# One addition of every output pair moved from VectorE to an accumulating DMA, the seven products of a pair reordered, and two weight loads moved ahead of the parameters

## The chip, the cores and the metric

The kernel runs on one core of a Trainium2 chip. The metric is the device time of one execution in microseconds (us). The kernel before takes 205.03 us, the median of three runs (203.96 to 205.6).

In profile lines PE is TensorE, PEld its weight loads, DVE is VectorE, ACT is ScalarE, POOL is GpSimd and SP is SyncE. A "q" behind the name (POOLq, SPq) is that engine's sequencer, which issues DMAs. L690 is line 690 of that kernel's own text, so the same statement can have different numbers in two kernels.

## The reference

Input x is 2048 tokens of 512 channels. Everything runs on its layer norm:

```python
xn  = layernorm(x)
u   = xn @ B_bar.T                     # complex, 512 states
h_t = Lam_bar * h_(t-1) + u_t          # scan over the 2048 tokens
y   = 2 * real(h @ C.T) + xn * Dskip
g   = silu(xn @ w1) * (xn @ w3)        # 1792 wide
out = x + y + g @ w2
```

The kernel works in four blocks of 512 tokens. A block has 14 tiles of gates (w1 and w3, called `glu`), 4 complex tiles of scan input (`bu`), and two output pairs. A pair is 256 tokens by 512 columns of the output. Gates and scan states are the contraction of one matrix product: 22 slices of 128.

## The kernel before

A pair is multiplied by a Strassen-like scheme: the left operand is cut into A11, A12, A21, A22 (128 tokens by 11 slices of 128, so 128x1408 each), and seven products of 11 matmuls of 256 columns replace eight. The price is four sums of left operands, each 128x1408, on VectorE:

```python
def row_sums(n, b, p):                       # cut
    return [(0.9, ... tensor_tensor(out=out, in0=x, in1=z, op=op), ("sums", n))
            for out, x, z, op in ((s1, a21, a22, ALU.add),        # S1 = A21 + A22
                                  (a21, a11, a21, ALU.subtract),  # S3 = A11 - A21
                                  (s2, s1, a11, ALU.subtract))]   # S2 = S1 - A11
```

The products, in program order (cut):

```python
def y_fast(n, then=()):
    mms(g, v["a11"], weight(0, D1), True)                 # 1  A11
    copy(f, g)
    bg.fill()
    mms(t, v["s1"], tsum[0], False, cols)                 # 2  S1, into PSUM tile t
    copy(q[1][:, cols], t)                                #    ScalarE takes it out
    bg.first(list(then))                                  #    the next pair's sums go to the front
    mms(f, v["a12"], weight(1, D1), False)                # 3  A12
    nc.vector.tensor_tensor(out=v["s4"], in0=v["a12"], in1=v["s2"], op=ALU.subtract)
    mms(g, v["s2"], tsum[1], False)                       # 4  S2
    mms(z, v["a22"], tsum[3], True)                       # 5  A22
    mms(t, v["s4"], weight(1, D2), False, cols)           # 6  S4, into tile t again
    product7()                                            # 7  S3
```

Between the products `bg.fill()` emits waiting VectorE tasks (sums, scans, scan products) as far as a simple count of TensorE's and VectorE's time allows. An argument of `bg.fill` holds VectorE's tasks back. `steps()` emits the next piece of a ScalarE list.

Near the first two pairs, the third block is made ready:

```python
def ln_scalar_engine(...):                     # layer norm of block 2 on ScalarE
    ...                                        # squares on ScalarE, then on GpSimd:
    gp.tensor_scalar(out=ss, ...)              #   L278
    gp.tensor_tensor(out=rstd, ..., op=ALU.pow)#   L279
    gp.tensor_tensor(out=nb, ...)              #   L280
  def norm(cl):
    nc.scalar.activation(out=xn_blk[b][:, cl, :], ...)    # L285, waits for L280
    ln_transpose(b, cl)                        # a DMA: xnT <- xn, four per block

def pre_c():                                   # scan input of the second block
    gp.dma_start(out=st["g"], in_=st["p"], accum_op=ALU.add)     # u <- p, 512 KB
```

And the head, in which the parameters of the scan are loaded ahead of the weights of the third and fourth gate tiles:

```python
load_w(0, 2 * P)
for i, src in enumerate((A_log_dt, A_Lambda_re, A_Lambda_im)):
    nc.sync.dma_start(out=par_rows[i * NPT:(i + 1) * NPT, :], in_=...)
load_w(2 * P, 4 * P)
```

## Time and profile before

| stretch of TensorE's program | us | length |
|---|---|---|
| head, to the first matmul of 512 columns | 0 to 13.47 | 13.47 |
| gates and scan inputs of blocks 1 and 2 | 13.47 to 70.45 | 56.98 |
| output pairs 0 and 1 ("the stretch" below) | 70.45 to 87.27 | 16.82 |
| gates of the third block to the last matmul | 87.27 to 200.08 | 112.81 |

The page of the kernel before, cut to its busy line, two of the slice rows (each digit is the busy tenths of 1/40 of the span; PEclk is the clock that TensorE was granted) and the two large DMA queues:

```profile
PE 198.3 (98%) x1317; PEld 122.8 (60%) x1317; DVE 172.7 (85%) x242; ACT 125.4 (62%) x251; POOL 39.0 (19%) x65
...
PEclk9999999999999999999999999999999999999999
DMA  6899999992573042926796004466330780101011
...
q1 hardware_dynamic: 25512, 13.21, 27.9%
q0 software_dynamic: 2592, 9.44, 24.9%
```

TensorE is busy for 198.3 of 203.1 us at full clock, VectorE for 85%. The view by windows, one row for each stretch of the table above (busy us of each engine, instructions in brackets; then granted clock, DMA share and GB/s):

```profile
13.47:70.45 56.98, 56.98 (x268) 25.83 (x265) 53.53 (x74) 52.13 (x101) 16.69 (x20) 1.00 0.75 164
70.45:87.27 16.82, 16.82 (x156) 15.06 (x155) 16.10 (x24) 13.30 (x34) 4.34 (x7) 1.00 0.57 110
87.27:200.08 112.81, 112.81 (x774) 73.64 (x771) 93.64 (x123) 51.63 (x96) 11.67 (x14) 1.00 0.38 76
```

In all three rows PE's busy time equals the length: there is nothing but matmuls. The waits of PE, longest first, of that profile (us in total, times, longest):

```profile
PE bu_ps L557 <- DMA w_sb<-in_B_w_dram: 1.0, 1, 1.0
PE bu_ps L193 <- PEq L883: 0.8, 1, 0.8
```

The only wait with a cause in the kernel's order is 1.0 us for weights in the head. Last, the timeline of GpSimd and then of ScalarE around the first pair (start, us, engine, line, operation, tiles; in brackets how long the engine had idled and for what):

```profile
72.55 0.89 POOL L468 DMA_DIRECT2D u<-p  x1 [3.21 <-DVE u L461]
74.73 0.80 POOL L278 TENSOR_SCALAR acc<-acc 128x4 f32<-128x4 f32 x1 [1.29 <-ACT xn L275]
75.61 1.05 POOL L279 TENSOR_TENSOR rstd_all<-acc,mhalf 128x4 f32<-128x4 f32 x1
76.74 0.25 POOL L280 TENSOR_TENSOR acc<-acc,rstd_all 128x4 f32<-128x4 f32 x1
80.42 0.93 POOL L468 DMA_DIRECT2D u<-p  x1 [3.43 <-DVE u L461]
```

```profile
73.56 0.36 ACT L744 ACTIVATE x_blk<-bu_ps 128x256 f32<-128x256 f32 x1
...
77.03 2.93 ACT L285 ACTIVATE xn<-x_blk,acc,rstd_all 128x512 bf16<-128x512 bf16 x4 [2.12 <-POOL acc L280]
```

GpSimd's chain L278, L279, L280 ends at 76.99, and the four layer norms of L285 start at once.

### The profile page before, as it was taken

What the parts mean: (1) busy time and instruction counts of PE and PEld (TensorE: products, weight loads), DVE (VectorE), ACT (ScalarE), POOL (GpSimd) and SP (SyncE); (2) the same over time, 40 slices, a digit from 0 to 9 for tenths busy, and PEclk for the clock granted to TensorE, in tenths of its full rate; (3) what the DMA queues carried; (4) which work ended last, traced back from release to release, by engine and by line L of the source; (5) the groups of instructions that cost most, each with busy time, mean ns of one, the idle gap of its engine ahead of it and who ended that gap; (6) DMA issues with size and microseconds to landing.
All of it is one profiled execution on the core that took longest, in us unless ns stands there. A gap on an engine that the chain in (4) does not pass through costs nothing.

```text
span 203.1 us, 3444 instructions
## 1 busy us (share of the span) xinstructions
PE 198.3 (98%) x1317; PEld 122.8 (60%) x1317; DVE 172.7 (85%) x242; ACT 125.4 (62%) x251; POOL 39.0 (19%) x65
## 2 busy tenths in 40 slices
PE   8899999999999999999999999999999999999994
PEld 2784444444444488854444445888444458888993
DVE  3779699999999999989949999999999935584832
ACT  4699897699999977959766676110566662101010
POOL 3250269700310143021111010310101110000000
PEclk9999999999999999999999999999999999999999
DMA  6899999992573042926796004466330780101011
GB/s 173 248 247 191 312 203 106 350 281 42 101 146 66 0 90 57 183 86 118 68 194 131 13 13 94 91 143 132 90 65 0 149 162 2 52 3 52 29 40 39
DMA packets 28696, 23.16 MB, mean 114 GB/s; under 512 B 16008, under 2 KB 26376, under 8 KB 28680
## 3 DMA queue, kind: packets, MB, share of 16 engines
q1 hardware_dynamic: 25512, 13.21, 27.9%
q0 software_dynamic: 2592, 9.44, 24.9%
q10 hardware_dynamic: 576, 0.30, 0.5%
q8 instruction: 10, 0.16, 0.3%
q14 instruction: 6, 0.05, 0.1%
HBM read 7.74 MB, written 2.10 MB: 48 GB/s over the span
## 4 chain that ended last, share of the span: by engine, by line
PE 93%; DMA 3%; SPq 2%; DVE 1%; issue 0%
PE gu_ps L525 45%; PE gu_ps L724 16%; PE y_ps L724 9%; PE bu_ps L724 7%; PE bu_ps L435 7%; PE y_ps L435 7%; DMA w_sb<-in_B_w_dram 3%; PE gu_ps L557 1%; PE bu_ps L557 1%; DVE xn L735 1%; SPq L166 0%; SPq L151 0%; SPq L161 0%; SPq L152 0%; DVE x_blk L735 0%
## 5 line engine op out<-in xcount | busy, mean ns | idle before, releaser
L525 PE MATMUL gu_ps<-xnT,w_sb 128*128 128x512 bf16 x424 | 92.5, 379 | 0.0
L525 PEld LDWEIGHTS <-w_sb 128*128 128x128 bf16 x424 | 41.4, 98 | 49.4
L724 PEld LDWEIGHTS <-act 128*128 128x128 f16 x451 | 43.2, 98 | 5.5
L534 ACT ACTIVATE g<-gu_ps 128x512 bf16<-128x512 f32 x55 | 33.1, 602 | 14.6 <-PE gu_ps L525 14.4
L535 ACT ACTIVATE u<-gu_ps 128x512 bf16<-128x512 f32 x55 | 33.2, 603 | 9.8 <-PE gu_ps L525 9.5
L543 DVE TENSOR_TENSOR act<-g,u 128x1024 f16<-128x1024 bf16 x28 | 19.0, 677 | 4.4 <-ACT u L535 4.4
L435 PEld LDWEIGHTS <-bt 128*128 128x128 bf16 x128 | 12.5, 98 | 15.1
L478 DVE TENSOR_TENSOR_SCAN u<-rho,act,u 128x512 bf16<-128x512 f32 x16 | 19.6, 1266 | 0.0
L492 POOL DMA_DIRECT2D act<-p x8 | 7.2, 900 | 45.8 <-DVE act L488 31.8
L435 PE MATMUL bu_ps<-xnT,bt 128*128 128x512 bf16 x64 | 15.1, 379 | 0.0
L435 PE MATMUL y_ps<-xnT,bt 128*128 128x512 bf16 x64 | 15.1, 379 | 0.0
L457 DVE TENSOR_TENSOR p<-u,tabe 128x2048 bf16<-128x2048 bf16 x8 | 9.8, 1219 | 2.6 <-DMA act<-p 2.5
L724 PE MATMUL y_ps<-tw,act 128*128 128x256 f16 x88 | 10.9, 272 | 0.0
L437 ACT ACTIVATE u<-y_ps 128x512 bf16<-128x512 f32 x16 | 9.5, 595 | 2.3 <-PE y_ps L435 2.1
L724 PE MATMUL gu_ps<-w_sb,act 128*128 128x256 bf16 (+1 forms) x84 | 10.8, 268 | 0.0
L724 PE MATMUL gu_ps<-tw,act 128*128 128x256 f16 x88 | 10.7, 273 | 0.0
L437 ACT ACTIVATE u<-bu_ps 128x512 bf16<-128x512 f32 x16 | 9.5, 595 | 2.0 <-PE bu_ps L435 1.9
L468 POOL DMA_DIRECT2D u<-p x6 | 5.3, 878 | 26.8 <-ACT u L535 7.9
L744 ACT ACTIVATE bu_ps<-y_ps 128x256 f32<-128x256 f32 x4 | 1.5, 369 | 13.7 <-PE y_ps L724 13.7
L461 DVE TENSOR_TENSOR u<-u,tabe 128x2048 bf16<-128x2048 bf16 x8 | 9.8, 1220 | 0.2
L478 DVE TENSOR_TENSOR_SCAN u<-rho,ends,u 128x512 bf16<-128x512 f32 x8 | 9.9, 1268 | 0.0
L484 DVE TENSOR_TENSOR p<-u,tabe 128x2048 f16<-128x2048 bf16 x8 | 9.8, 1221 | 0.1
(143 smaller groups left out, 275.1 us busy)
## 6 DMA issues: line engine op xcount, KB each, us to landing
act<-p POOLq DMA_DIRECT2D x8, 512.0 KB, 4.7
u<-p POOLq DMA_DIRECT2D x6, 512.0 KB, 4.7
xn<-x_blk POOLq DMA_DIRECT2D x4, 512.0 KB, 5.6
out_dram<-xn SPq DMA_DIRECT2D x15, 128.0 KB, 1.7
w_sb<-in_B_w_dram SPq DMA_DIRECT2D x1, 1792.0 KB
x_blk<-in_A_x_dram SPq DMA_DIRECT2D x3, 512.0 KB, 9.0
w_sb<-in_B_w_dram SPq DMA_DIRECT2D x2, 768.0 KB, 7.1
w_sb<-in_B_w_dram SPq DMA_DIRECT2D x4, 256.0 KB, 3.7
```

The lines of the kernel that those rows point to most:

```text
L435: nc.tensor.matmul(out=ps, lhsT=bt[:, ri, dt, pt * P:(pt + 1) * P], rhs=xnT_blk[b][:, dt, :], start=(dt == 0), stop=(dt == NDT - 1))
L437: nc.scalar.activation(out=u[:, j, ri, :], in_=ps, func=ACT.Copy)
L457: nc.vector.tensor_tensor(out=st["p"][:, :, ::-1, :], in0=st["g"], in1=tabe[:, psl, 2:0:-1, :], op=ALU.mult)
L461: nc.vector.tensor_tensor(out=st["g"], in0=st["g"], in1=tabe[:, psl, 0:1, :].to_broadcast(FULL), op=ALU.mult)
L478: nc.vector.tensor_tensor_scan(out=v, data0=rho[:, pt:pt + 1].to_broadcast([P, TBLK]), data1=v, initial=init, op0=ALU.mult, op1=ALU.add)
L484: nc.vector.tensor_tensor(out=st["p16"][:, :, ::-1, :], in0=st["g"], in1=tabe[:, psl, 1:3, :], op=ALU.mult)
L492: gp.dma_start(out=act_state(b, hf), in_=st["p16"], accum_op=ALU.add)
L525: nc.tensor.matmul(out=ps[:, tsl], lhsT=w[:, dt, f * P:(f + 1) * P], rhs=xnT[:, dt, tsl], start=(dt == 0), stop=(dt == NDT - 1))
L534: nc.scalar.activation(out=g16[:, f % 2, :], in_=g_ps, func=ACT.Silu)
L535: nc.scalar.activation(out=u16[:, f % 2, :], in_=u_ps, func=ACT.Copy)
L543: nc.vector.tensor_tensor(out=act(b)[:, k0:k1 + 1:k1 - k0, :], in0=g16, in1=u16, op=ALU.mult)
L724: nc.tensor.matmul(out=out, lhsT=left[:, k, :], rhs=right[k][:, cols], start=(start and k == 0), stop=(k == NK - 1), skip_group_check=True)
```

## The change

The intent is to take one of the sums from VectorE: S1 = A21 + A22 is made in place of A21 by an accumulating DMA. S3 then needs a place of its own, S2 = A22 - S3, and the product of S1 moves to the fifth place so that its DMA has time. The second part moves two weight loads ahead of the parameters, and TensorE's work on those weights ahead of the parameters' transpose. With them comes a hold-back: over the last three gate tiles of the second, third and fourth block VectorE's waiting tasks are put off. Cut to its core:

```diff
@@ head
     load_w(0, 2 * P)
+    load_w(2 * P, 4 * P)
     for i, src in enumerate((A_log_dt, A_Lambda_re, A_Lambda_im)):
         nc.sync.dma_start(out=par_rows[...], ...)
-    load_w(2 * P, 4 * P)
@@ first block: quarters of the first gate tiles
             quarter(0, (0, 1), 2)
+            quarter(1, (0, 1)); ln_first_transpose(2); quarter(0, (2,)); quarter(1, (2,))
             pps = params_transpose() ... table_angles(1)
-            quarter(1, (0, 1)); ln_first_transpose(2); quarter(0, (2,)) ... quarter(1, (2,))
@@ gates: the hold-back
-            bg.fill()
+            bg.fill(-0.7 if b > 0 and f >= NFT - 3 else None)
@@ row_sums
-    S1, S3, S2 on VectorE
+        return [(0.9, subtract(s3, a11, a21), ("sums", n)),
+                (0.0, lambda: gp.dma_start(out=a21, in_=a22, accum_op=ALU.add), ("sums", n)),
+                (0.9, subtract(s2, a22, s3), ("sums", n))]
@@ y_fast: order of the products
-    A11, S1, A12, S2, A22, S4, S3   (last pair: S3 before S4)
+    A11, A22, A12, S2, S1, S3, S4
@@ before the first pair
+    bg.flush(("ends", 0))
```

## The prediction

> **What bounds the kernel now.** TensorE. The page gives PE 198.3 of 203.1 us at a granted clock of 1.00, and the chain of waits is one unbroken run of matmuls from 9.89 to 198.87 us: 112 matmuls of 512 columns in 24.17 us (216 ns each), 11 of 256 columns in 1.20 us (109 ns). By windows, PE is busy in all of 9.85 to 198.9 us. VectorE is 85% busy but PE never waits for it there. Two places are not matmul: the head, where PE waits 1.0 us (8.88 to 9.89 us) for the third gate tile's w3 weights, and the tail after 198.87 us.
>
> **What the change does.** PE has the same 2636 instructions, so the matmul floor stays. VectorE loses one 128x1408 operation of 0.88 us for each of 8 output pairs, 7 us in all; eight accumulating DMAs of 352 KB from GpSimd replace them, about 4 us each, an estimate from the existing 512 KB ones (4.7 us to landing). The Trainium skill ("DMA: Bandwidth & Descriptors", SWDGE vs HWDGE vs iDMA) says that accumulation is possible only from GpSimd; this trace agrees, all 9.44 MB of it is in the software queue q0. S1's product moves from second to fifth place of seven, 4.8 us into a pair, so the DMA has 6 us or more of slack. VectorE's 7 us are off the critical path: worth nothing.
>
> **Head.** Three small issues (about 1.1 us) leave the SyncE queue ahead of the two weight loads, so the w3 load should land near 8.7 us in place of 9.85 and the 1.0 us wait should shrink to 0 to 0.3 us. But the parameters are now transposed after quarter (1,2), and kr, rho and the 1.28 us table load hang on them: par, dtv, kr, rho, table, first Silu. I put that Silu at 12.1 us (12.56 before), so the first 512-column matmul, which needs its buffer, starts at about 12.9 against 13.47 us. Gain 0.5 us.
>
> **Where it can be given back.** (1) Pair 0: the copy of S1's product now has one product's time before S4 reuses that PSUM, and stands on ACT behind a normalisation that waits for POOL (77.0 us): 0 to 0.4 us. (2) The start of the third block's gates (87.3 us): its last transposes of xn land at about 86.7 us, delayed by an accumulating DMA that fills the 16 DMA engines from 82 to 85 us (DMA share 0.97 to 1.04). The change puts both of that block's accumulations later and two stores ahead of the fourth transpose: 0 to 1 us of wait.
>
> Sum: -0.5, +0.2, +0.3, and 1 and 2 may stay zero: about -0.4 us.
>
> **Prediction: 204.5 us, 8 in 10 between 203.4 and 205.9. Faster by over 2%: 0.01; within 2%: 0.965; slower by over 2%: 0.025.**
>
> **What would show it.** Right: PE's wait for w_sb in the head gone or under 0.3 us, first 512-column matmul at 12.7 to 13.2 us; DVE busy about 166 us; PE busy unchanged within 1 us; no PE wait for the S1 DMA. Wrong: waits of PE for ACT near 77 us, or for xnT near 87 us, over 0.5 us each; a wait of PE for par_rows near 9.4 us.
>
> **What would make it wrong.** Parameters landing after 10 us behind the weights in the same rings; the S1 DMA queueing behind other accumulations by over 6 us; VectorE running late in a pair, since S3's product now waits for an addition with one product's time.

## The result, and the profile after

The changed kernel takes 209.94 us (median of six runs, 209.45 to 211.63) beside 204.5 us (203.85 to 205.6, six runs) of the kernel before. The ratio is 1.0282, 95% interval 1.0226 to 1.0338: slower. Here and below a ratio is the mean time of one kernel's fast runs over that of the other's fast runs of the same rounds, so it is not quite the ratio of the quoted medians. Executions over 1.5% slower than the fastest of the same kernel are left out of the means.

The page after, the same lines as before:

```profile
PE 200.8 (97%) x1317; PEld 124.0 (60%) x1317; DVE 166.6 (80%) x234; ACT 124.8 (60%) x251; POOL 56.3 (27%) x73
...
PEclk9999999999999995799999999999999999999999
DMA  5999995991789068950639784299970087982911
...
q0 software_dynamic: 13984, 12.32, 43.0%
```

VectorE lost 6.1 us of work as intended, the software queue q0 (GpSimd's DMAs) rose from 24.9% to 43.0%, and the clock row, all nines before, has a 5 and a 7 between 78 and 88 us. The three stretches by windows:

```profile
12.43:69.41 56.98, 56.98 (x265) 25.82 (x264) 54.32 (x77) 51.69 (x101) 20.85 (x28) 1.00 0.84 171
69.41:92.25 22.84, 19.87 (x156) 16.58 (x155) 14.41 (x24) 13.30 (x34) 7.59 (x9) 0.85 0.77 98
92.25:205.06 112.81, 112.81 (x774) 73.68 (x771) 91.00 (x118) 51.68 (x96) 23.85 (x20) 1.00 0.63 95
```

The first and the third row are the same to 0.01 us. The stretch of the first two pairs grew from 16.82 to 22.84 us. PE's busy time in it, 19.87 in place of 16.82, says that 3.05 us of that are slower matmuls, and 22.84 - 19.87 = 2.97 us are idle. The head gave 13.47 - 12.43 = 1.04 us in this pair of profiles, so the sum is 6.02 - 1.04 = 4.98 us, against 208.0 - 203.1 = 4.9 us of the spans. The largest wait of PE:

```profile
PE bu_ps L730 <- ACT x_blk L750: 3.0, 1, 3.0
```

Timelines of GpSimd and ScalarE at that place:

```profile
73.03 1.95 POOL L690 DMA_DIRECT2D act<-act  x1 [4.76 <-DVE tw L687]
75.06 1.26 POOL L278 TENSOR_SCALAR acc<-acc 128x4 f32<-128x4 f32 x1
76.40 1.90 POOL L279 TENSOR_TENSOR rstd_all<-acc,mhalf 128x4 f32<-128x4 f32 x1
78.38 0.20 POOL L280 TENSOR_TENSOR acc<-acc,rstd_all 128x4 f32<-128x4 f32 x1
78.60 0.95 POOL L468 DMA_DIRECT2D u<-p  x1
```

```profile
78.61 0.81 ACT L285 ACTIVATE xn<-x_blk,acc,rstd_all 128x512 bf16<-128x512 bf16 x1 [5.02 <-POOL acc L280]
79.33 0.36 ACT L750 ACTIVATE x_blk<-bu_ps 128x256 f32<-128x256 f32 x1
```

The DMA of S1 of the second pair (L690) takes GpSimd 1.95 us to issue, where the u<-p of the kernel before took 0.89. Behind it stands the chain of the layer norm, which ends at 78.58 in place of 76.99. The issue is only a part of that: ScalarE's squares were done at 73.32, so the chain started 1.7 us late behind the issue, and its three steps then took 3.52 us from start to end in place of 2.26. Steps of the same length follow the issue in e3, e4 and e15; why they are longer was not tested. ScalarE waits for the chain with L285, and the copy of S1's product (L750) stands behind that in ScalarE's program. TensorE needs the copied PSUM tile for S4. Then the clock, in windows of 2 us (the DMA share counts the whole time of each packet where it starts, so that a short window can show more than 1):

```profile
77.00:79.00 2.00, 0.00 (x0) 0.00 (x0) 0.73 (x2) 0.39 (x1) 1.90 (x3) 0.97 1.42 106
79.00:81.00 2.00, 1.26 (x7) 0.89 (x7) 0.75 (x2) 2.00 (x4) 0.55 (x1) 0.50 0.59 103
81.00:83.00 2.00, 2.00 (x11) 1.45 (x10) 0.71 (x2) 0.81 (x2) 0.00 (x0) 0.50 0.97 166
83.00:85.00 2.00, 2.00 (x11) 1.42 (x10) 0.84 (x1) 0.37 (x2) 0.86 (x1) 0.50 2.00 70
85.00:87.00 2.00, 2.00 (x17) 1.65 (x15) 0.00 (x0) 2.00 (x8) 0.00 (x0) 0.82 0.93 188
```

TensorE is granted half its clock (0.50) from 78.88 to 85.71 us by the trace's clock records (the expectation of e4 below says 85.3): it is "busy" in these rows and does half the work. The clock fell during the wait, 2.1 us after the last matmul had ended at 76.77, and TensorE resumed at 79.74.

A second delay is hidden in this trace. The four transposes of the third block's xn landed 2.8, 2.4, 5.2 and 4.4 us after their issue before, and take 7.0, 5.5, 6.2 and 3.8 us now; the last lands at 91.4 us in place of 86.7 (the landings that `prof` does not list are read from the semaphore updates in the traces). The gates that need them start at 92.25, so nobody waits. But had the pairs kept their 16.82 us, the gates would have been due at 69.41 + 16.82 = 86.23 us and would have waited up to 5 us, an estimate that leaves the landings where they are.

### The profile page after: what moved, and what is told of

It reads as the page before. It is cut to its first block, busy times and chain, and to the rows that moved or that the text cites. A ratio compares the mean times of both kernels' runs of the same rounds, so it can differ in the third digit from the quotient of the medians.

```text
span 208.0 us, 3442 instructions
## 1 busy us (share of the span) xinstructions
PE 200.8 (97%) x1317; PEld 124.0 (60%) x1317; DVE 166.6 (80%) x234; ACT 124.8 (60%) x251; POOL 56.3 (27%) x73
## 2 busy tenths in 40 slices
DMA packets 40088, 26.04 MB, mean 125 GB/s; under 512 B 27400, under 2 KB 37768, under 8 KB 40072
## 4 chain that ended last, share of the span: by engine, by line
PE 62%; DVE 14%; POOL 9%; issue 8%; DMA 4%; ACT 0%; POOLq 0%
PE gu_ps L525 23%; PE gu_ps L730 16%; PE y_ps L730 7%; PE bu_ps L730 7%; PE bu_ps L435 3%; PE y_ps L435 3%; DMA xn<-x_blk 3%; DVE act L543 2%; DVE stats L214 2%; DVE tw L663 1%; DVE tw L371 1%; DMA x_blk<-in_A_x_dram 1%; DVE ct L397 1%; PE gu_ps L557 1%; POOL act L690 1%
## 5 line engine op out<-in xcount | busy, mean ns | idle before, releaser
L730 PEld LDWEIGHTS <-act 128*128 128x128 f16 x462 | 45.0, 101 | 10.0 <-issue 3.1
L690 POOL DMA_DIRECT2D act<-act x8 | 15.8, 1975 | 23.9 <-DVE tw L687 13.8
L730 PE MATMUL bu_ps<-w_sb,act 128*128 128x256 bf16 (+3 forms) x98 | 13.0, 275 | 3.0 <-ACT x_blk L750 3.0
L730 PE MATMUL gu_ps<-w_sb,act 128*128 128x256 bf16 (+3 forms) x112 | 14.9, 275 | 0.0
L770 DVE TENSOR_TENSOR act<-act,tw 128x1408 f16<-128x1408 f16 x4 | 3.6, 892 | 10.0 <-PE gu_ps L730 8.4
```

The source lines that it names most:

```text
L690: (0.0, lambda: gp.dma_start(out=a21, in_=a22, accum_op=ALU.add), ("sums", n)),
L730: nc.tensor.matmul(out=out, lhsT=left[:, k, :], rhs=right[k][:, cols], start=(start and k == 0), stop=(k == NK - 1), skip_group_check=True)
```

## The experiments

All 18 kernels gave correct results. "Stretch" is from the first product of pair 0 to the first gates of the third block, "rest" from there to the end of the last matmul; both are from one profile. The time is the median of all runs (four each, six for e17, and six of before and of after); the ratio takes the fast ones alone (three each for e5 and e9). All profiled runs were fast, but for e5, whose profiled run is 2% above its fastest and counts as slow: its two lengths and its waits are of that run.

| run | what it is | us | ratio to before (95%) | stretch | rest |
|---|---|---|---|---|---|
| before | | 204.5 | 1 | 16.82 | 112.81 |
| after | the whole change | 209.94 | 1.028 (1.023 to 1.034) | 22.84 | 112.81 |
| e1 | before + head | 205.2 | 1.004 (1.000 to 1.008) | 18.08 | 112.82 |
| e2 | after, S1 of pair 1 issued late | 213.3 | 1.042 (1.034 to 1.049) | 25.18 | 114.45 |
| e3 | after, norms behind the copy | 210.8 | 1.030 (1.025 to 1.035) | 22.31 | 114.51 |
| e4 | after + 28 useless matmuls | 209.14 | 1.023 (1.019 to 1.026) | 21.21 | 112.82 |
| e5 | after, S1 of pair 1 on VectorE | 208.99 | 1.018 (1.011 to 1.025) | 21.27 | 114.51 |
| e6 | after, every S1 on VectorE | 212.06 | 1.037 (1.033 to 1.040) | 22.57 | 114.51 |
| e7 | e5 + GpSimd held 6.9 us | 212.82 | 1.040 (1.038 to 1.043) | 24.91 | 112.82 |
| e8 | e6 with the old head | 208.73 | 1.020 (1.015 to 1.026) | 20.19 | 114.41 |
| e9 | after without hold-back | 209.78 | 1.026 (1.021 to 1.030) | 21.51 | 112.83 |
| e10 | before + hold-back | 205.68 | 1.004 (1.001 to 1.008) | 17.32 | 112.82 |
| e11 | e8 without hold-back | 206.64 | 1.010 (1.009 to 1.012) | 17.76 | 113.93 |
| e12 | before, parameters from GpSimd | 205.14 | 1.003 (1.002 to 1.005) | 16.81 | 112.82 |
| e13 | last six pairs changed, rest before | 204.26 | 1.001 (0.998 to 1.004) | 16.81 | 112.81 |
| e14 | e13 + new head | 205.43 | 1.006 (1.003 to 1.009) | 17.96 | 112.83 |
| e15 | first two pairs changed, rest before | 209.39 | 1.025 (1.021 to 1.029) | 21.78 | 112.82 |
| e16 | e13, VectorE held 6 copies in the head | 205.35 | 1.006 (1.003 to 1.008) | 16.98 | 112.83 |
| e17 | e13 + e12 | 205.04 | 1.004 (1.002 to 1.006) | 16.82 | 112.81 |
| e18 | e13, VectorE held 8 copies | 206.4 | 1.008 (1.006 to 1.011) | 18.16 | 112.82 |

The theory at the outset: GpSimd's long issue delays the layer norm, which delays the copy, which stops TensorE, and the half clock doubles the loss. The rivals: the reordering alone, the head, or the DMA traffic does it.

### e1: the head alone

The edit to the kernel before is the first two hunks of the diff above.

> The kernel before with only the head of the change (weight loads ahead of the parameters, quarters reordered). All theories: the head's share of the change is a gain, since in the trace of the changed kernel the first 512-column matmul starts at 12.43 us against 13.47 us. Expected 1.0 us faster than before: about 203.5 us where before has 204.5, no PE wait for w_sb over 0.3 us, nothing else moved.

205.2 us, ratio 1.004. The wait for w_sb fell to 0.3 us, but new waits came later: 0.7 us for VectorE's S4 subtraction (L766), which starts at 75.7, and 0.2 us for xnT at 87.6. So the head alone is far from the 5 us, and its own gain is gone. e14, e16 and e18 come back to this.

### e2: the DMA of S1 issued behind the layer norm's chain

```diff
+        if late:                 # in y_fast, after the product of A22
+            late()
-    y_fast(0, row_sums(1, *pairs[1]))
+    second = row_sums(1, *pairs[1])
+    y_fast(0, (second[0], second[2]), second[1][1])
```

> The changed kernel with one instruction moved: the accumulating DMA for the second pair's S1 is issued behind the three small POOL operations of the normalisation, not ahead of them. Theory A (POOL's queue: 1.95 us of issuing ahead of the normalisation, the copy of S1's product waits on ACT behind that normalisation, PE waits 3 us and its clock halves for 6 us): PE's wait near 77 us falls from 2.97 us to under 0.3 us, the granted clock stays 1.0, about 203.5 to 204.5 us. Rival B (the accumulating DMAs cost by their traffic and descriptor writing wherever they are issued): stays within 1 us of 209.9 us. Rival C (the new order of products as such): stays at 209.9 us.

213.3 us, the slowest of all. The wait for the copy shrank from 3.0 to 0.8 us, as the theory has it, but TensorE now waits 2.9 us for the S1 DMA itself and 2.5 us for xnT, with half clock after both. The issue can't be moved a few microseconds back without meeting its own deadline.

### e3: the norms behind the copy in ScalarE's program

```diff
-    ln_scalar_engine(2, ..., sins, (0, 1, 4))
+    ln_scalar_engine(2, ..., sins, (0, 1, 5))
```

> The changed kernel with the four normalisations one step later in ACT's program, so that the copy of S1's product stands ahead of them; POOL's order is as in the change. Theory A: PE's wait near 77 us gone although POOL's chain still ends near 78.4 us; but the normalised rows of the third block come as late as in the change while PE arrives 5 us earlier, so PE may wait up to 1.5 us for xnT near 86 us: 203.5 to 205.5 us. Rival B: POOL and the DMA engines as busy as before, so 208 us or more. Rival C: 209.9 us.

210.8 us, not better. PE's waits in this run:

```profile
PE gu_ps L525 <- DMA xnT<-xn: 2.8, 1, 2.8
PE gu_ps L730 <- ACT gu_ps L750: 1.7, 1, 1.7
...
PE y_ps L730 <- DVE x_blk L741: 0.5, 1, 0.5
```

The 3.0 us wait behind the norm is gone; 2.8 us for xnT, 1.7 us for the next copy and 0.5 us for an addition on VectorE stand in its place. The copy's place was a limit, but not the only one.

### e4: TensorE kept at work during the wait

```diff
         for t, cols in halves:
+            # n == 0 only, ahead of the S4 product
+            for _ in range(28):
+                nc.tensor.matmul(out=f, lhsT=ones[:, 0:P], rhs=ones[:, 0:DH], start=True, stop=True)
```

> The changed kernel with 28 useless matmuls of 256 columns (3.05 us at full clock) on PE just ahead of S4's product of the first pair, where PE idles 2.97 us. If the half clock from 79 to 85.3 us comes from that idle time, the clock stays at 1.0 and the half-speed loss of about 3.1 us goes: about 206.8 us. If the clock drops for a reason that has nothing to do with the idle time, 209.9 us. The result stays correct: the matmuls write a PSUM tile that is read no more.

The clock stays at 1.0, yet only about 0.8 us of the 3 us come back: 209.14 us. Two rows of the windows of 2 us:

```profile
80.00:82.00 2.00, 2.00 (x20) 1.67 (x18) 0.78 (x3) 2.00 (x5) 0.39 (x1) 1.00 0.65 119
82.00:84.00 2.00, 2.00 (x21) 1.80 (x19) 1.54 (x2) 1.46 (x4) 0.16 (x1) 1.00 0.98 171
```

In this profile the stretch is 1.6 us shorter than in the change: the useless matmuls fill 3.3 us, and the xnT wait, hidden before, shows with 1.0 us from 90.4. The head of this profile is 0.7 us longer, of the size of its scatter. The half clock is shown as a consequence of the idle time, and the second limit stands close behind it.

### e5, e6, e8: S1 back on VectorE

```diff
-   (0.0, lambda: gp.dma_start(out=a21, in_=a22, accum_op=ALU.add), ("sums", n)),
+   (0.0, lambda: nc.vector.tensor_tensor(out=a21, in0=a21, in1=a22, op=ALU.add), ("sums", n)),
    # e5: for n == 1 only; e6: for all pairs; e8: for all pairs, with the old head
```

> The changed kernel with the S1 of the second pair alone added on VectorE in place; the seven other S1 stay accumulating DMAs. Revised theory: that one DMA does the harm, by holding POOL's queue for 1.95 us ahead of the normalisation and by filling the DMA engines ahead of the two scan accumulations and the transposes of xn. Then PE's wait near 77 us is under 0.5 us, xnT is there near 88 us, clock 1.0, 204 to 206 us. Rival (the harm is spread over all eight DMAs, or lies in the new order): 208 us or more.

> The changed kernel with all eight S1 added on VectorE in place, order of products and head as in the change. If the other seven DMAs are harmless, this equals the run with the second pair alone within 0.5 us, 204 to 206 us. If they cost too, it is over 1 us faster than that run. If VectorE's 0.88 us per pair matters in the new order, it is slower.

> The new order of products alone: all S1 on VectorE, head of the kernel before. If the order as such is harmless it is within 0.7 us of before (204.5 us); if it costs, over 206 us.

e5 has no long issue on GpSimd in the stretch: the wait for the copy is gone, but xnT is waited for 3.6 us. e6 has no S1 DMA at all and is slower than the change itself, 212.06 us, with waits of 4.0 us for xnT and 1.5 us for an addition on VectorE. e8, without the new head, takes 208.73 us:

```profile
PE gu_ps L525 <- DMA xnT<-xn: 2.2, 1, 2.2
PE bu_ps L730 <- ACT x_blk L750: 0.8, 1, 0.8
```

So the DMA isn't the one cause. The order of the products with the hold-back is enough for a loss of 2%, and even with GpSimd's chain on time (ended at 77.08) the copy behind the norm costs 0.8 us. Why the new head makes e6 3 us slower than e8 was followed up only for the head by itself (below).

### e7: GpSimd held without a DMA

```diff
+   hold = [(0.0, lambda: [gp.tensor_copy(out=junk, in_=s3[:, k, :]) for k in range(9)], ...)]  # n == 1
-   return [(0.9, subtract(s3, a11, a21), ("sums", n)),
+   return [(0.9, subtract(s3, a11, a21), ("sums", n)), *hold,      # and S1 of pair 1 on VectorE
```

> As the run with the second pair's S1 on VectorE, with nine small POOL copies [...]where that DMA's issue stood: POOL is held as by the DMA, without its traffic. If POOL's queue is what counts, PE waits near 77 us for 2 to 3 us again, the clock falls, 208 to 210 us. If the traffic in the DMA engines counts, no such wait, 204 to 206 us.

```profile
73.12 6.90 POOL L690 COPY junk<-tw 128x128 f16<-128x128 f16 x9 [4.53 <-DVE tw L688]
...
81.51 0.20 POOL L280 TENSOR_TENSOR acc<-acc,rstd_all 128x4 f32<-128x4 f32 x1
```

```profile
PE bu_ps L733 <- ACT x_blk L753: 5.0, 1, 5.0
```

The copies were meant to hold GpSimd as long as the DMA's issue. They hold it for 6.9 us, far longer than that issue, so the size of the loss is not the change's. What it shows is the chain: with the norm's chain ended at 81.7, the wait for the copy grew to 5.0 us, with no DMA of S1 in pair 1. GpSimd's time is what TensorE waits for there.

### e9, e10, e11: the hold-back

```diff
-            bg.fill(-0.7 if b > 0 and f >= NFT - 3 else None)      # e9: taken out of after
+            bg.fill()                                              # e11: taken out of e8
# e10: the reverse, put into the kernel before
```

> The changed kernel without its hold-back of VectorE's background work over the last three gate tiles of a block (that line as before). Theory D, formed after the runs on the new order: the hold-back and the new order move the third block's first scan accumulation from 72.6 to 78 us, on top of the transposes of xn, which then land near 90 us in place of 86.7. If so, that accumulation is issued before 73 us again, xnT lands by 88 us, PE's wait for it is under 1 us, and the time is 204.5 to 206.5 us, although all eight S1 DMAs are there. Theory A alone (S1's DMA on POOL) also gives a low time, since POOL's order changes too; the new order as such gives 208 us or more.

> The kernel before with the hold-back line alone. Theory D: the first scan accumulation of the third block is issued near 75 us in place of 72.6, the transposes land later, PE waits 1 to 3 us for xnT near 87 us: 205.5 to 208.5 us. If the hold-back is harmless by itself: within 0.7 us of before.

> The run with the new order alone (S1 on VectorE, head of before; 208.7 us) without the hold-back. Theory D: within 1 us of before, 204 to 205.5 us. If the order of products is the cause rather than when the accumulation is issued: it stays at 207 to 209 us.

By itself the hold-back costs 0.4% (e10). Without it the change stays at 1.026 (e9): u<-p is issued at 72.6 again and the copy is in time, but PE waits 1.6 us for VectorE's addition, 0.8 us for the S1 DMA and 1.9 us for xnT. The new order without hold-back and without DMA (e11) costs 1.0%, in two waits for the same addition on VectorE, one in the first pairs and one in a later pair at 132 us:

```profile
PE gu_ps L730 <- DVE x_blk L741: 1.0, 1, 1.0
PE y_ps L730 <- DVE x_blk L741: 0.8, 1, 0.8
```

The wait for xnT is gone in e11 (2.2 us in e8, which differs by the hold-back alone): the third block's first u<-p is issued at 71.96 us in place of 77.32. The prediction named the wait for VectorE as a risk: in the new order S3's product stands right behind S1's, and the addition that frees its PSUM tile has one product's time. The parts do not add up: e11 +1.0%, with hold-back +2.0% (e8), with hold-back and head +3.7% (e6), with the DMAs too +2.8% (after).

### e12: the parameters on another queue

```diff
-    for i, src in enumerate((A_log_dt, A_Lambda_re, A_Lambda_im)):     # ahead of load_w(2 * P, 4 * P)
-        nc.sync.dma_start(out=par_rows[...], ...)
+        nc.gpsimd.dma_start(out=par_rows[...], ...)                    # after affine_select on GpSimd
```

> The kernel before, with only the three parameter loads moved from SyncE's queue to GpSimd's, early. The weights of the third and fourth gate tiles are then issued 1.1 us earlier as in the change, and the parameters are not later, so that VectorE's angle tables do not start later (9.1 us before; 10.7 us with the change's head). Expected: PE's wait for w_sb gone, first 512-column matmul near 12.5 us; 0.3 to 1.0 us faster than before, limited by xnT near 87 us: 203.5 to 204.3 us. If the head's gain is always given back at xnT: same as before.

The wait for w_sb is gone and TensorE runs from 12.35 to 198.96 us without a gap, 1.1 us earlier than before. Even so the span is 203.2 us and the time 205.14: the end of the kernel after the last matmul took 4.3 us in place of 3.0. Its last stores landed late; why was not settled. e17 shows the same.

### e13 and e15: which pairs carry the loss

Both kernels hold the old and the new text of `row_sums` and `y_fast` and choose by pair; both have the old head.

```diff
+    def y_fast(n, then=()):
+        return (y_fast_old if n < 2 else y_fast_new)(n, then)      # e13; e15 has n >= 2
-            bg.fill(-0.7 if b > 0 and f >= NFT - 3 else None)
+            bg.fill(-0.7 if b > 1 and f >= NFT - 3 else None)      # e13; e15 has b == 1
```

> The last six pairs as in the changed kernel (six S1 sums by accumulating DMA, new order, hold-back in the third and fourth block), the first two pairs and the head as before. Theory (all of the loss lies in the stretch of the first two pairs, the rest costs nothing): third block's gates at 86.8 to 87.5 us, from there to the last matmul 112.8 us, 204 to 205.3 us, ratio 0.998 to 1.003. Rival (the six late DMAs or the late order cost something that was hidden behind the earlier delay): over 113.5 us from the gates to the last matmul, 206 us or more, and a PE wait for a DMA or a sum after 130 us.

> The first two pairs as in the changed kernel (their two sums, one of them after the start of the stretch, by DMA; new order; hold-back in the second block), the last six pairs and the head as before. Theory (all of the loss lies here): first 512-column product of the pairs to the third block's gates about 22 us in place of 16.8, 209 to 211 us, ratio 1.022 to 1.033. Rival (the late pairs carry part of it): under 207 us.

```profile
69.60:86.41 16.81, 16.81 (x155) 15.07 (x154) 16.18 (x24) 13.30 (x34) 4.39 (x7) 1.00 0.56 110
86.41:199.22 112.81, 112.81 (x774) 73.72 (x771) 89.54 (x117) 51.69 (x96) 23.43 (x21) 1.00 0.65 95
```

```profile
69.90:91.68 21.78, 18.80 (x156) 15.83 (x154) 14.48 (x24) 13.20 (x34) 8.28 (x9) 0.92 0.78 102
91.68:204.50 112.82, 112.82 (x772) 73.70 (x772) 95.00 (x123) 51.63 (x96) 11.62 (x14) 1.00 0.38 76
```

The first two rows are of e13, the others of e15. They settle where the loss lies. With six S1 DMAs, the new order and the hold-back in the last six pairs, the 112.81 us from the third block's gates on are unchanged and the ratio is 1.001. With the change in the first two pairs alone the stretch takes 21.78 us (18.80 busy, so 1.98 us of slower matmuls; 2.98 us idle) and the ratio is 1.025 of the change's 1.028. PE's waits in e15 are those of the change:

```profile
PE bu_ps L744 <- ACT x_blk L764: 2.7, 1, 2.7
...
PE gu_ps L525 <- DMA xnT<-xn: 0.3, 1, 0.3
```

### e14, e16, e18: the head once more

e14 is e13 with the new head. e16 and e18 are e13 with the old head and six or eight useless copies on VectorE ahead of its first angle table:

```diff
+            for _ in range(6):                                     # e18: 8
+                nc.vector.tensor_copy(out=slot32[NPT], in_=iota_f)
             table_angles(0)
```

> The same with the new head. Theory (the head's gain is about 0.3 us and is partly given back at the third block's gates): 203.7 to 205.2 us, ratio 0.996 to 1.003. Rival (the head's microsecond is real and survives where the first two pairs are not delayed): 203.3 us or less, ratio 0.994 or less.

> e13 (old head, late pairs changed) with six useless copies on VectorE ahead of the first angle table, so that VectorE alone starts its tables as late as with the new head (about 10.7 to 11.2 us in place of 9.5) while TensorE's head stays as it is. Theory (the new head costs what it costs through VectorE, which is busy from there to 78 us and can't catch up): VectorE's subtraction for S4 near 75.1 to 75.8 in place of 73.8 us, a PE wait for it of 0.3 to 1.0 us, the stretch of the first pairs 17.2 to 18.2 in place of 16.8 us, 204.7 to 205.8 us. Rival (the order of quarters or the loads cost it, not VectorE): no PE wait there, stretch 16.8, time as e13, 204.2 to 204.6 us.

> e16 with eight copies in place of six. In e16 VectorE's subtraction for S4 came 4.9 us after TensorE's first product of the pairs (4.2 in e13, 5.9 in e14 and e1), and no wait of PE showed, so e16 held too little to decide. With two copies more, 0.94 us, it should come 5.6 to 5.9 us after it. Theory (VectorE's lateness alone makes PE wait): a PE wait of 0.3 to 1.0 us for that subtraction near 75.7 us, as in e14 and e1, stretch of the first pairs 17.3 to 18.2 us, 205.3 to 206.3 us. Rival: no such wait, stretch 16.8 to 17.0 us, and VectorE has slack there.

The new head costs e13 1.2 us by the medians of the same chip (205.43 against 204.26). The subtraction for S4 on VectorE in e14, and PE's wait for it:

```profile
75.69 0.88 DVE L873 TENSOR_TENSOR act<-act,x_blk 128x1408 f16<-128x1408 f16 x1
```

```profile
PE bu_ps L831 <- DVE act L873: 0.6, 1, 0.6
```

In e13 that subtraction started at 73.80, that is 4.2 us after the first product of pair 0, and in e14 5.9 us after it. The cause is at the start: with the new head the parameters come later, and VectorE's first angle table starts at 11.09 in place of 9.48 us. VectorE is busy for 19.5 of the 20 us from 50 to 70 us and does not catch up.

e16 is inconclusive: the time, 205.35 us, is what the theory expected, but VectorE came only 4.9 us after the first product and no wait of PE showed. e18 held it for two copies more. It came 6.1 us after the first product, and the wait is there, 0.9 us, the stretch 18.16 us:

```profile
PE bu_ps L833 <- DVE act L875: 0.9, 1, 0.9
```

So VectorE's lateness alone makes TensorE wait. The head of that profile was late as well (first 512-column matmul at 13.41, with waits for w_sb that add up to 0.8 us), so e18's 206.4 us are not all due to the later wait, and lie a little over the expected range.

### e17: the last candidate

e13 with the parameters on GpSimd's queue, as in e12; both edits are shown above.

> e13 with the parameters loaded from GpSimd's queue as in e12: the weights leave SyncE early and VectorE's tables still start by 9.1 us. Theory: no wait of PE between the weights' arrival and the last matmul (first 512-column matmul 12.3 to 12.6, stretch 16.8, then 112.8 us), last matmul ended by 199.2 us, 203.6 to 204.6 us, ratio 0.995 to 1.001. Rival (what the tail took back in e12 is lost again or more): 204.7 us or over. A version that beats the kernel before by 2% is not expected.

205.04 us. No wait after the head, and again a tail of 4.0 us from the last matmul to the end of the span (3.0 in e13). No version beats the kernel before; e13 equals it.

## Why the prediction was wrong

The prediction was 204.5 us, within 203.4 to 205.9; the change takes 209.94. Slower by over 2% had been given 0.025. Point by point:

- **What bounds the kernel**: right. TensorE's matmuls, with VectorE's removed work worth nothing by itself: e13 removes the S1 sums of six pairs from VectorE and takes the same time.
- **The S1 DMA has 6 us or more of slack**: right for the change as it stands, where nothing waits for it (e2 and e9, which move the schedule, do wait 2.9 and 0.8 us). Its landing took 6.6 us, not the estimated 4.
- **Head, 0.5 us gained**: the local part was right, the wait for w_sb went to 0.3 us or less in all profiles with the new head but one (0.6 in e4). The gain was of the size of the scatter: the first 512-column matmul starts at 12.89 us on average in six profiles with the old head (12.46 to 13.47) and at 12.69 in ten with the new one (12.43 to 13.13). And it was given back: VectorE's tables start later, and TensorE waits for VectorE at 76.0 us in e14 and 76.6 in e18. "VectorE is 85% busy but PE never waits for it there" was true, but the slack was about 1 us there: in the kernel before the subtraction starts 4.1 us after the first product, in e14 5.9 us after it, and TensorE waits 0.6.
- **(1) The copy behind the norm, "0 to 0.4 us"**: this is the step that failed. Place and mechanism were right, the size was 2.97 us of waiting and 3.05 us of half clock behind it, 6.0 us in all. Two terms were left out. GpSimd's queue: the prediction kept the norm's chain at its old 77.0 us, but the issue of the DMA stands ahead of the chain that the copy waits for, it took 1.95 us and not the 0.9 of the other accumulations, the chain started 1.7 us late behind it, and its steps took 1.3 us longer. And the clock: the sum of waits has no term for what an idle TensorE costs after it. Even the wait by itself was sized short: with GpSimd's chain ahead of that issue or without the issue (e2, e8) it is still 0.8 us. So some 2.2 of the 2.97 us go with the issue and the slower steps behind it, an estimate from these three waits.
- **(2) The transposes for the third block's gates, "0 to 1 us"**: the mechanism fits (e11 against e8 for the time of the accumulation), the size was short. The wait is 1.0 to 4.0 us in e3, e4, e5, e6, e8 and e9, where the first limit is lifted or smaller. In the change itself it is covered by (1).
- **The sum of parts**: wrong as a method here. The stretch holds several chains (GpSimd's norm and the copy, accumulations and transposes on the DMA engines, VectorE's additions) with little slack each. Taking any one away shows the next, which is why e3, e5 and e9 win at most 1%.

What stays open: why the new head makes e6 3 us slower than e8; why the tail of e12 and e17 is 1 us longer; and why L278 and L279 on GpSimd took 1.26 and 1.90 us in place of 0.80 and 1.05 in the change.

## What to carry to other kernels

Moving work off an engine that is not the limit can pay only with slack, and costs wherever the replacement goes: look at what stands behind a new DMA issue in that engine's queue, and follow it until it reaches the limiting engine. Price a long wait of TensorE with the clock that comes after it, which doubled the loss here: after the head, every wait of 2.2 us or more in these traces went with half clock, and none of 1.9 us or less. When a stretch has several chains close to the limit, change the parts of the program that have slack (here the last six pairs) and leave that stretch alone, or expect the parts' costs not to add up.

## What the Trainium skill lacked or had wrong

- "TensorE: Matmul & The Clock Gate", Part 1 and "Why this matters for your kernels": it puts the fall to half clock after an idle window of about 3.4 us and advises against gaps over about 3 us. In e8 a wait of 2.2 us (88.0 to 90.3) was enough, with a clock of 0.5 from 90.1 to 93.5; in e9 1.9 us and in e4 1.0 us were not. The page does say that the window runs free; the half rate itself agrees. How long it lasts did not follow the wait: 6.8 us with 3.0 us idle in the change, but 3.4 us with 2.7 us in e15 and with 4.0 us in e6.
- "DMA: Bandwidth & Descriptors", "Where the ~2 µs actually goes": descriptor generation is called small and variable. The issue of the S1 DMA (352 KB, 1408 rows of 256 bytes; the eight of them raised the count of packets under 512 B from 16008 to 27400) held GpSimd 1.95 us, that of a 512 KB accumulation 0.90 us, and this was on the critical path.
- The same page, "Why small descriptors are slow (HBM only)": transfers within SBUF are said not to suffer. The S1 DMA stays within SBUF; from the shares of q0, (0.430 x 208.0 - 0.249 x 203.1) / 8 = 4.9 us of all 16 engines for 352 KB, against 0.249 x 203.1 / 18 = 2.8 us for an existing 512 KB accumulation. Both accumulate; no plain copy of short rows was run.
- The same page, "Issuing engines are not separate DMA queues": it says that all run on the same 16 engines and interleave. The size is missing: the third block's four transposes, issued from SyncE, took 5.6 us to landing on average in the change, with GpSimd's accumulations later and one of S1 ahead of them, against 3.7 us before.
